# New due times, leads and leanings for a planned order of the same operations: a state-space convolution beside Hedgehog linear attention

## The chip, the cores and the metric

The kernel runs on one core of a Trainium2 chip. The core has four engines that compute, each with its own in-order queue: TensorE (PE, with its weight loads shown apart as PEld), VectorE (DVE), ScalarE (ACT) and GpSimd (POOL). SyncE (SP) issues all of this kernel's transfers, in order. The metric is the device time of one execution in microseconds (us).

## What is computed

Two heads work on inputs of 2048 rows and 576 columns, and their results stand side by side. Head A is an S4D convolution: a filter K for each of 576 channels, made from 128 complex exponentials, convolved over the length with u by a Fourier transform. Head B is Hedgehog linear attention with 32 heads of 18 columns.

```python
# A
dt = jnp.exp(log_dt)
A = -jnp.exp(log_A_real) + 1j * A_imag
C = (C_real + 1j * C_imag) * dt[:, None]
P = jnp.exp((A * dt[:, None])[:, :, None] * pos[None, None, :])
K = 2.0 * jnp.einsum("dn,dnl->dl", C, P).real
y = jnp.fft.irfft(jnp.fft.rfft(u_t, L2) * jnp.fft.rfft(K, L2)[None], L2)[:, :, :L]
a = y.transpose(0, 2, 1) + u * D_skip[None, None, :]
# B
q, k, v = x @ wqkv, split in heads
pq, pk = q and k of each head times w_phi
phi = concatenate([softmax(p), softmax(-p)])          # for pq and pk
kv, z = phi_k^T v, sum over rows of phi_k
o = (phi_q kv) / (phi_q z + 1e-6)
b = o as (rows, 576) @ wo
```

## The kernel before

The work is cut in units, and a planner puts the operations of all units in one order. The units are:

- **fold** 0 and 2: the key's and the query's projection multiplied with w_phi (five blocks, through tiles named e, E and kvb); fold 1 and 3: wv and wo (three parts each; wo's through three tiles e). Each part is loaded, copied to a rounded half wh by ACT (L497, L513) and its rest to wl by DVE or POOL (L498, L514).
- **key** 0 to 15: 128 rows each. The rows are loaded and split (steps without a name, and xd, which stores the split rows for later), multiplied with the folded weights (PE, L431, the helper that records every matmul), passed through the two softmaxes (DVE L568 to L582, POOL L579, ACT L576; step k1, k2) and accumulated into a PSUM tile (k3, k4). **kv** turns the sum into the operand of the queries.
- **query** 0 to 15: the split rows are read back (L536), multiplied, passed through the softmaxes (step q1, q2), transposed (q3), multiplied with kv and divided (q4), transposed again (q5) and multiplied with wo (q6).
- **u** 0 to 15: the first step of the transform of u (u1), kept in DRAM. It takes a tile zi.
- **mags**, **sel**, **par** 0 to 5: the filter's parameters. **group** 0 to 17: two groups of 16 channels each. POOL makes phases (L883 to L888), ACT their sine and cosine (step g1; L898, L903, L904), PE and ACT the magnitudes (g2; L918), DVE multiplies them in (g3; L924 to L929), PE makes the filter (g4) into a tile ks.
- **kfirst** 0 to 3: the first step of the transform of a quarter of the filter, through four tiles zi, stored to DRAM (L950). A quarter needs nine groups.
- **product** 0 to 15: eight for each half of the channels. It loads ff (L988), ub (L995), fk and kb (L1016, L1018), transforms u (p1), multiplies with the filter's transform (p2, p3) and transforms back (p4), storing to DRAM (L1054). The products of a half need all of u and two quarters of the filter.
- **last** 0 to 15: eight for each half. It loads a tile zi (L1064), which needs every product of its half, makes the last step of the transform (l1) and stores the result (L1078).

The planner knows an estimated cost of each operation and walks forward in time. Among the operations that are ready for an engine it takes the one that is due first; the due time of an operation is that of its unit in WANT less the LEAD of its step (the sixth entry of an operation), so a larger LEAD means earlier:

```python
self.ops.append([eng, cost, fn, deps, bufs, self.now - early - LEAD.get(self.part, 0.0), table, ...])
key = (s + late if s + late > at[e] + NEAR else at[e], ops[k][5] + (STAY if e == "pe" and ops[k][10] != mode else 0.0), k)
```

NEAR is the time within which a start counts as at once. STAY is added to the due time of a matmul that needs another tiling of PE than the last one had; TURNOVER to the start of an ACT operation that needs another function table. Some operations may go to either of two engines ("any": ACT or DVE; others DVE or POOL): the engine that ends it first is taken, with LEAN_ACT or LEAN_POOL added to DVE's end.

Tiles come from tags with few buffers. For all but PSUM a tag is strict: its tiles are ranked by the due times of the operations that use them, and a tile may not take a buffer that one of an earlier rank still needs.

```python
for k in sorted(range(n), key=lambda k: ops[k][5]):
    for b in ops[k][4]:
        if id(b) not in place:
            place[id(b)] = seen[b.tag]
...
before = p - low[tag] - more
if before >= self.window[tag]:
    return None
if before and self.strict[tag] and before - sum(v < p for v in ahead[tag]) >= len(fr):
    return None
```

The tags that matter here: zi has 2 buffers (fold 1, u, kfirst, last), e has 3 (the parts of fold, the softmaxes of keys and queries), v1 2 (keys, the parts of sel), x9 3 (the split rows). Where the planner foresees that PE would wait, it puts filler matmuls on a zero tile in front of the next one (L215), so that PE's clock stays up.

Of the kernel before, what the change touches and what calls it, by code (L numbers as in the profile page):

```python
# [158 lines left out]
class Plan:  # L159
# [26 lines left out]
    def op(self, eng, cost, fn, r=(), w=(), with_=(), early=0.0, table=None, busy=1.0, lock=False, mode=(128, 128), add=None):  # L186
# [16 lines left out]
        fill = [add] if add else fill  # L203
        self.ops.append([eng, cost, fn, deps, bufs, self.now - early - LEAD.get(self.part, 0.0), table, busy, lock and eng, (self.unit, early, self.part), mode, fill[0] if fill else None, alt, add])

# [170 lines left out]
def c_dma(nbytes, run=4096):  # L376
# [3 lines left out]


FLEX = "dve", "pool"
STAY, TURNOVER, NEAR, LEAN_POOL, LEAN_ACT = 2.8232, 86.2691, 108.9723, -101.9467, 54.4707
LEAD = dict(g1=890.9031, g2=620.0778, g3=192.8580, g4=207.1228, k1=216.0814, k2=-118.1697, k3=-65.4639, k4=-547.2126, l1=-1073.5691, p1=-946.0003, p2=-42.8734, p3=-112.1202, p4=-277.0577, q1=6.7377, q2=-167.0245, q3=-16.4915, q4=-253.9455, q5=-371.4825, q6=-501.1500, u1=950.3189, xd=-230.4561)
FILL = 114.0


WANT = dict(
    ident=[1001.5195],
    fold=[-6117.3543, -7207.7506, -340.8826, -248],  # L390
    start=[-3485.651],
    key=[-5200.524, -857.2856, -3283.7984, -2041.2554, -2036.0389, -1264.7043, -10155.3465, -4286.2764, -2911.8045,
          -2558.4292, -1360.1364, -2657.9782, -3095.7741, -2082.143, -907.5394, -211.7701],
    kv=[-444.8623],
    query=[1690.5431, 4124.6299, 4143.7194, 1995.4459, 2673.1544, 2389.5478, 1349.1511, 3409.721, 207.6882, 445.7265,
          3385.202, 806.1601, 2667.4484, 3524.0524, 3569.4059, 3651.1724],
    u=[-2745.6629, -420.1168, 204.104, -1422.0066, -3363.2519, 366.0833, -11691.5594, -445.6771, -220.033, -1000.4812,
          -1001.382, -3135.6904, -1460.411, -4014.0618, -2618.6448, 469.9849],
    mags=[-6043.0357],
    sel=[-7319.891, -11916.8894, -3931.5985],  # L400
    dsk=[331.8456],
    par=[-7693.8238, -4634.0292, -1718.349, 81.9699, 1301.2247, 2220.1341],
    group=[-4512.8072, -5429.8639, -4985.5845, -4145.1561, -2678.7949, -1878.2961, -914.9546, -2232.1852, -1467.543,
          -90.2167, -293.4502, -856.2089, 82.9071, 239.3902, 1222.1458, 1540.0762, 1647.3815, 309.0567],
    kfirst=[-2505.5117, -1015.4687, -401.9894, 856.7455],
    product=[1228.5589, 1255.9756, 1206.883, 59.9875, 440.7206, -16.8928, 1079.6264, 659.7095, 1486.7365, 2093.1899,
          2182.0643, 1480.5801, 3075.8325, 2134.1925, 2348.2184, 2387.2577],
    last=[1039.7028, 583.559, 59.784, 2209.6938, 1958.6146, 1737.3942, 2116.436, 1850.9013, 2710.0021, 2371.1266,
          2120.546, 2972.9234, 2398.2107, 3055.0304, 2543.6038, 2544.8052],
)  # L410


# [694 lines left out]
```

## Time and profile before

| | us |
|---|---|
| median of three runs | 597.67 |
| the three runs | 593.55, 597.67, 597.73 |
| the profiled execution | 596.77 |
| its span, first to last instruction | 595.0 |

All rows of the profile are of that one execution. In a row of groups stands the line, engine, operation, tiles (written <- read), shapes and count, then the busy time and mean duration, then the idle time ahead of it and what ended it. In a row of windows stands the window, then busy time (and count) of PE, PEld, DVE, ACT and POOL, the granted share of PE's clock, the DMA engines' busy share and GB/s. In the chain of waits and in a timeline stands the start, the duration and what ran.

### The profile page before, as it was taken

The page shows a single profiled execution, that of the slowest core. Times are in us where ns is not written, and L with a number is a line of the kernel's source. Part 1 is how long each engine was busy: PE and PEld are TensorE (multiplying, and loading weights), DVE is VectorE, ACT ScalarE, POOL GpSimd, SP SyncE. Part 2 cuts the span into 40 slices and gives each one's busy share as a digit, 9 for nine tenths or more (in the row PEclk, how much of TensorE's full clock was granted, in tenths as well). Part 3 has the DMA queues.
Part 4 walks back from the last instruction along what each step waited for, and adds up shares of the span by engine and source line. Part 5 has one row for each costly group of instructions (what it writes and reads, how often), then busy time and mean ns, then how long its engine had stood idle before and what let it go on. Part 6 is the DMA issues. An engine that isn't in the chain of part 4 may idle for free.

```text
span 595.0 us, 19001 instructions
## 1 busy us (share of the span) xinstructions
PE 566.4 (95%) x7794; PEld 468.6 (79%) x7794; DVE 517.7 (87%) x1106; ACT 385.8 (65%) x663; POOL 252.4 (42%) x397
## 2 busy tenths in 40 slices
PE   4999989999999998999999999999999999999996
PEld 3998889999978687898786876766787966777974
DVE  4799899999999996899999999899996789677751
ACT  4479766679596987669668586986965434432332
POOL 0438376685762825943462448545710122011100
PEclk9899999999999999999999999999999999999999
DMA  8979912542048697025666746876529799997687
GB/s 264 280 249 310 332 43 64 191 131 89 9 161 219 196 298 200 1 92 140 190 221 202 254 122 207 239 243 216 156 51 309 188 308 341 308 296 259 198 240 200
DMA packets 91317, 119.26 MB, mean 200 GB/s; under 512 B 9826, under 2 KB 73186, under 8 KB 91230
## 3 DMA queue, kind: packets, MB, share of 16 engines
q1 hardware_dynamic: 91230, 118.04, 63.9%
q8 instruction: 61, 1.00, 0.7%
q14 instruction: 26, 0.21, 0.1%
HBM read 68.76 MB, written 49.26 MB: 198 GB/s over the span
## 4 chain that ended last, share of the span: by engine, by line
PE 63%; DVE 18%; DMA 12%; ACT 3%; issue 2%; SPq 1%; POOL 1%; ACTq 0%; DVEq 0%
PE ps L431 57%; DMA zi<-dram 3%; PE ps L215 3%; DVE ac L450 2%; PE ps L678 2%; DVE cs L924 2%; DMA zo<-in_xT_dram 2%; DVE E L925 2%; DMA e<-in_wo_dram 2%; DMA e<-in_wqT_dram 1%; DMA e<-in_wkT_dram 1%; DVE E L927 1%; DVE E L929 1%; DVE e L446 1%; DMA out_dram<-yo 1%
## 5 line engine op out<-in xcount | busy, mean ns | idle before, releaser
L431 PE MATMUL ps<-wh,x 128*128 128x288 f32 (+2 forms) x1008 | 241.3, 320 | 4.0 <-DMA x<-xd 2.1
L431 PEld LDWEIGHTS ps<-wh,x 128*128 128x128 f32 x1008 | 173.3, 189 | 15.9 <-issue 4.3
L431 PE MATMUL ps<-wl,x 128*128 128x288 f32 (+2 forms) x560 | 175.1, 313 | 0.0
L888 POOL TENSOR_TENSOR cs<-cs,pi 128x128 int32<-128x128 int32 (+4 forms) x180 | 118.5, 661 | 10.1
L431 PEld LDWEIGHTS ps<-wl,x 128*128 128x128 f32 x560 | 105.8, 189 | 0.5
L579 POOL TENSOR_TENSOR o<-e 128x576 f32<-128x576 f32 x32 | 43.1, 1350 | 60.7 <-ACT e L576 54.8
L918 ACT ACTIVATE ps<-ps 128x512 f32<-128x512 f32 x108 | 56.5, 582 | 5.3 <-PE ps L431 5.0
L446 POOL TENSOR_TENSOR ac<-ac 128x288 f32<-128x288 f32 x28 | 22.3, 803 | 75.2 <-DVE ac L450 75.1
L924 DVE TENSOR_TENSOR cs<-ps,cs 128x1024 f32<-128x1024 f32 x36 | 43.7, 1213 | 5.1 <-ACT ps L918 4.8
L215 PE MATMUL ps<-ident,zero 128*32 128x256 bf16 (+6 forms) x330 | 42.9, 281 | 2.7 <-DVE ident L464 1.6
L450 DVE TENSOR_TENSOR ac<-us,ps 128x576 f32<-128x576 f32 x64 | 44.6, 746 | 1.0 <-ACT fT L436 0.5
L431 PEld LDWEIGHTS ps<-kvb,fT 126*128 126x128 f32 (+1 forms) x320 | 38.6, 188 | 6.5 <-issue 2.2
L925 DVE TENSOR_TENSOR E<-ps,cs 128x1024 f32<-128x1024 f32 x36 | 43.5, 1208 | 0.0
L431 PEld LDWEIGHTS ps<-E,cs 128*32 128x32 f32 x2304 | 34.9, 110 | 10.3 <-issue 4.0
L431 PE MATMUL ps<-E,cs 128*32 128x64 f32 x2304 | 41.3, 221 | 1.5 <-DVE E L929 1.0
L431 PE MATMUL ps<-kvb,fT 126*128 126x133 f32 (+1 forms) x320 | 41.5, 279 | 0.7 <-DVE small L571 0.7
L576 ACT ACTIVATE e<-e 128x1152 f32<-128x1152 f32 x32 | 37.1, 1172 | 7.4 <-DVE e L446 6.8
L904 ACT ACTIVATE cs<-cs,hp 128x1040 f32<-128x1040 f32 x36 | 41.4, 1149 | 0.0
L898 ACT ACTIVATE cs<-cs 128x1040 f32<-128x1040 int32 x29 | 31.2, 1074 | 14.9 <-POOL cs L888 14.8
L436 ACT ACTIVATE ot<-ps 128x288 f32<-128x288 f32 x28 | 11.5, 411 | 44.5 <-PE ps L431 44.4
L215 PEld LDWEIGHTS <-zero 128*32 128x32 bf16 (+6 forms) x330 | 32.1, 102 | 10.2 <-issue 4.2
L568 DVE TENSOR_REDUCE small<-ps 128x16 f32<-128x288 f32 (+2 forms) x64 | 28.7, 449 | 12.0 <-PE ps L431 11.2
(140 smaller groups left out, 1077.9 us busy)
## 6 DMA issues: line engine op xcount, KB each, us to landing
xd<-x SPq DMA_DIRECT2D x16, 576.0 KB, 6.0
dram<-zi SPq DMA_DIRECT2D x16, 576.0 KB, 3.8
x<-xd SPq DMA_DIRECT2D x16, 576.0 KB, 4.4
dram<-zi SPq DMA_DIRECT2D x32, 288.0 KB, 3.4
kb<-dram SPq DMA_DIRECT2D x32, 288.0 KB, 4.6
ub<-dram SPq DMA_DIRECT2D x32, 288.0 KB, 3.9
dram<-zo SPq DMA_DIRECT2D x32, 288.0 KB, 4.3
zi<-dram SPq DMA_DIRECT2D x16, 576.0 KB, 5.2
```

What stands on the lines that cost most here:

```text
L215: self.matmul(t[0:cols, 0:n], self.zero.t[0:rows, 0:cols], self.data.t[0:rows].bitcast(BF16)[:, 0:n], start=not o[13], stop=not o[13], ski ...
L431: pe.matmul(o, l, r, start=start, stop=stop, skip_group_check=skip)
L450: op(eng, c_dve(n) if eng == "dve" else c_pool(n), lambda: e.tensor_tensor(dst(), a(), b(), op=alu), r=r, w=w, lock=eng == "pool" or not a ...
L568: op("dve", c_dve(DH * m), lambda: dve.tensor_reduce(ends.t[:, :, 0], v(), axis=AX.X, op=ALU.max, negate=True), r=[p], w=[ends])
L576: op("act", c_act(1152) + 40, lambda: act.activation(e.t, e.t, AF.Exp), r=[e], w=[e], table="exp")
L579: op("pool", c_pool(470), lambda: pool.tensor_tensor(pair.t, e.t[:, :, :, 0:9], e.t[:, :, :, 9:18], op=ALU.add), r=[e], w=[pair], lock=True)
L888: op("pool", c_pool(2 * n * W), lambda n=n, j=j: pool.tensor_tensor(x()[:, :, :, n:2 * n], x()[:, :, :, 0:n], pi.t[:, j:j + 2, gs].bitcast ...
L898: op(("act", "dve"), (c_act(65 * W), c_dve(65 * W)), lambda e, cs=cs, x=x: act.activation(cs.t[:, 0], x(), AF.Abs) if e == "act" else dve. ...
L904: act.activation(cs.t[:, 0], cs.t[:, 0], AF.Sin, scale=-TURN, bias=hp.t)
L918: op("act", c_act(512), lambda: act.activation(ps.t, ps.t, AF.Exp), r=[ps], w=[ps], table="exp")
L924: op("dve", c_dve(64 * W), lambda: dve.tensor_tensor(F(), both(M.t), F(), op=ALU.mult), r=[M, cs], w=[cs])
L925: op("dve", c_dve(64 * W), lambda: dve.tensor_tensor(E.t[:, :, :, 32:64], both(up.t), cs.t[:, :, :, 0:32], op=ALU.mult), r=[up, cs], w=[E])
```

## The change

The program's operations stay the same. Other values are put in for STAY, TURNOVER, NEAR, the two leanings, all LEADs and all due times in WANT.

```diff
--- before.py
+++ after.py
@@ -380,33 +380,33 @@
 
 
 FLEX = "dve", "pool"
-STAY, TURNOVER, NEAR, LEAN_POOL, LEAN_ACT = 2.8232, 86.2691, 108.9723, -101.9467, 54.4707
-LEAD = dict(g1=890.9031, g2=620.0778, g3=192.8580, g4=207.1228, k1=216.0814, k2=-118.1697, k3=-65.4639, k4=-547.2126, l1=-1073.5691, p1=-946.0003, p2=-42.8734, p3=-112.1202, p4=-277.0577, q1=6.7377, q2=-167.0245, q3=-16.4915, q4=-253.9455, q5=-371.4825, q6=-501.1500, u1=950.3189, xd=-230.4561)
+STAY, TURNOVER, NEAR, LEAN_POOL, LEAN_ACT = 37.6104, 135.5510, 109.2559, -92.0902, 57.9818
+LEAD = dict(g1=1412.5796, g2=445.7536, g3=858.8018, g4=859.8314, k1=227.1989, k2=29.9342, k3=83.2118, k4=-331.8215, l1=-1032.4912, p1=-505.0832, p2=172.0822, p3=6.0949, p4=-304.5765, q1=56.1909, q2=-209.9832, q3=-272.1636, q4=-311.2748, q5=-352.9193, q6=-792.7688, u1=840.3076, xd=385.3628)
 FILL = 114.0
 
 
 WANT = dict(
-    ident=[1001.5195],
-    fold=[-6117.3543, -7207.7506, -340.8826, -248],
-    start=[-3485.651],
-    key=[-5200.524, -857.2856, -3283.7984, -2041.2554, -2036.0389, -1264.7043, -10155.3465, -4286.2764, -2911.8045,
-          -2558.4292, -1360.1364, -2657.9782, -3095.7741, -2082.143, -907.5394, -211.7701],
-    kv=[-444.8623],
-    query=[1690.5431, 4124.6299, 4143.7194, 1995.4459, 2673.1544, 2389.5478, 1349.1511, 3409.721, 207.6882, 445.7265,
-          3385.202, 806.1601, 2667.4484, 3524.0524, 3569.4059, 3651.1724],
-    u=[-2745.6629, -420.1168, 204.104, -1422.0066, -3363.2519, 366.0833, -11691.5594, -445.6771, -220.033, -1000.4812,
-          -1001.382, -3135.6904, -1460.411, -4014.0618, -2618.6448, 469.9849],
-    mags=[-6043.0357],
-    sel=[-7319.891, -11916.8894, -3931.5985],
-    dsk=[331.8456],
-    par=[-7693.8238, -4634.0292, -1718.349, 81.9699, 1301.2247, 2220.1341],
-    group=[-4512.8072, -5429.8639, -4985.5845, -4145.1561, -2678.7949, -1878.2961, -914.9546, -2232.1852, -1467.543,
-          -90.2167, -293.4502, -856.2089, 82.9071, 239.3902, 1222.1458, 1540.0762, 1647.3815, 309.0567],
-    kfirst=[-2505.5117, -1015.4687, -401.9894, 856.7455],
-    product=[1228.5589, 1255.9756, 1206.883, 59.9875, 440.7206, -16.8928, 1079.6264, 659.7095, 1486.7365, 2093.1899,
-          2182.0643, 1480.5801, 3075.8325, 2134.1925, 2348.2184, 2387.2577],
-    last=[1039.7028, 583.559, 59.784, 2209.6938, 1958.6146, 1737.3942, 2116.436, 1850.9013, 2710.0021, 2371.1266,
-          2120.546, 2972.9234, 2398.2107, 3055.0304, 2543.6038, 2544.8052],
+    ident=[662.8542],
+    fold=[-7687.5453, -7745.6125, 259.817, 535.0881],
+    start=[-2611.6173],
+    key=[-6803.1211, -230.1406, -1365.6963, -2159.2507, -2013.4955, -1452.8544, -2939.3499, -2827.6947, -5050.6309,
+          -2518.8535, -2118.4827, -2650.666, -9070.313, -995.7874, -2373.4398, -987.9414],
+    kv=[-786.7682],
+    query=[3770.3533, 3016.2205, 509.4875, 2846.8004, 1491.4103, 3693.7243, 3988.4128, 4713.0274, 1842.5362,
+          2601.4694, 2059.0315, 4163.9131, 979.8723, 550.1266, 4637.1683, 3978.4516],
+    u=[-2652.5344, -1884.6824, -2759.9008, -2536.1968, -519.4906, -1715.5344, 61.2931, -1133.0048, -3905.8435,
+          -3179.3226, -79.6233, -3423.2365, -3284.4628, -4491.6778, -2694.6224, -12210.2772],
+    mags=[-6932.6723],
+    sel=[-4531.7687, -13025.2225, -9048.6714],
+    dsk=[-1454.0969],
+    par=[-8082.5413, -6080.3201, -1900.8545, 318.5964, 1347.4086, 2335.0621],
+    group=[-5429.9062, -5502.1674, -5990.1496, -4902.2989, -4185.1114, -2837.5423, -3314.4141, -2894.5059, -2718.3579,
+          -1748.4322, -1071.7324, -831.957, -412.4379, 1066.8302, 1224.9381, 1181.0338, 1103.1102, 2326.0027],
+    kfirst=[-3805.4915, -1483.2884, -573.9485, 1243.6831],
+    product=[1234.4685, -154.0236, 1747.233, 70.1659, 1226.8661, 949.6933, 49.7659, 1059.5957, 2418.1186, 3443.8845,
+          3102.0019, 2360.5039, 2005.2384, 3993.9616, 1947.1217, 2343.6319],
+    last=[873.1326, -129.3535, 2214.046, 737.0179, 504.8954, 188.1562, 1822.1782, 642.4446, 4235.0692, 3659.2532,
+          3501.5163, 3991.4065, 3676.1068, 2821.8987, 3937.8348, 3122.3667],
 )
 
 
```

## The prediction

> **What bounds the kernel now.** I read the page first (busy shares, slices, chain), then busy time by windows cut where the slices change, then the fillers, the chain of waits in order of time, and last the timelines of SP, PE and DVE at the places where the chain leaves PE and DVE.
>
> ```profile
> span 595.0 us, 19001 instructions
> PE 566.4 (95%) x7794; PEld 468.6 (79%) x7794; DVE 517.7 (87%) x1106; ACT 385.8 (65%) x663; POOL 252.4 (42%) x397
> DVE  4799899999999996899999999899996789677751
> DMA  8979912542048697025666746876529799997687
> PE 63%; DVE 18%; DMA 12%; ACT 3%; issue 2%; SPq 1%; POOL 1%; ACTq 0%; DVEq 0%
> ```
>
> The sum below is made against this execution: 596.77 us with a span of 595.0, 0.9 below the median of 597.67 us. PE looks full everywhere, but part of that is filler. The next answer gives the busy time of the filler matmuls alone (PE, PEld, DVE, granted clock, DMA share, GB/s), the one after it that of all work:
>
> ```profile
> 0.00:75.00 75.00, 11.63 (x79) 8.70 (x79) 0.11 (x1) 0.95 0.90 288
> 75.00:450.00 375.00, 29.97 (x242) 22.60 (x242) 0.00 (x0) 1.00 0.52 158
> 450.00:595.00 145.00, 1.33 (x9) 0.84 (x9) 0.00 (x0) 0.99 0.84 265
> ```
> ```profile
> 0.00:14.20 14.20, 6.66 (x42) 5.01 (x42) 6.44 (x18) 7.18 (x11) 0.79 (x10) 0.94 0.85 259
> 14.20:75.00 60.80, 60.73 (x486) 55.60 (x487) 52.67 (x132) 44.74 (x74) 29.50 (x45) 0.96 0.91 295
> 75.00:225.00 150.00, 144.81 (x2553) 128.77 (x2552) 145.89 (x287) 111.88 (x181) 91.92 (x146) 1.00 0.46 140
> 225.00:250.00 25.00, 22.30 (x247) 20.23 (x250) 19.13 (x39) 17.66 (x27) 17.53 (x20) 1.00 0.36 101
> 250.00:456.00 206.00, 200.00 (x3041) 158.89 (x3031) 199.89 (x416) 156.15 (x260) 97.74 (x164) 1.00 0.60 185
> 456.00:557.00 101.00, 99.78 (x1201) 73.69 (x1202) 77.34 (x180) 36.07 (x88) 12.29 (x12) 1.00 0.87 277
> 557.00:595.00 38.00, 32.08 (x247) 26.42 (x245) 16.36 (x41) 12.15 (x25) 2.62 (x2) 0.97 0.72 212
> ```
>
> So there are three regimes. Up to 75 us transfers feed a full PE. From 75 to 456 us DVE is the limit: it idles 4.1 us in 75 to 225 (150 - 145.89), 5.9 us in 225 to 250 and 6.1 us in 250 to 456, while PE runs 30 us of filler. From 456 us on (the last group of the filter is done there) PE is the limit, with hardly any filler, and DVE idles 23.7 us, then 21.6 us. An order of the same operations cannot shorten the work; it can only take idle time from DVE before 456 us, or move PE work from after 456 us into the time that filler takes now.
>
> **What the new numbers change.** I sorted the due times of both versions by hand (WANT less the LEAD of the part) and looked at what buffers with a strict order (zi 2, e 3, v1 2, x9 3) make of them, since a tile there may not be taken ahead of one that is due earlier.
>
> *The start.* Before: sel 1, u 6, key 6, par 0, sel 0, fold 1, fold 0, mags, group 1, key 0. After: sel 1, u 15, key 12, sel 2, par 0, fold 1, fold 0, mags, key 0. Units of one kind are alike, so this is one order under other names. In zi, six u units stand ahead of kfirst 0, seven more ahead of kfirst 1 and three ahead of kfirst 2, in both versions. The third part of sel is fifth in v1 in both. PE's long wait stays as it is:
>
> ```profile
> PE ps L431 <- DMA e<-in_wkT_dram: 6.0, 1, 6.0
> ```
>
> Cost 0, between -1 and +1.
>
> *The fold of wo.* Before, fold 3 (-248) takes its three e tiles ahead of every query, the first of which is due at 201 (208 - 6.7). After, query 2 (509 - 56 = 453) and query 13 (494) come ahead of fold 3 (535). The hole at 225 to 250 us is made of this:
>
> ```profile
> 220.73 10.62 DMA e<-in_wo_dram
> POOL wl L514 <- ACT wh L513: 6.8, 2, 4.4
> 224.50 0.46 DVE L568 TENSOR_REDUCE small<-ps 128x16 f32<-128x288 f32 x1 [0.17 <-PE ps L431]
> 232.87 0.46 DVE L450 TENSOR_TENSOR e<-ps,small 128x288 f32<-128x288 f32 x1 [2.94 <-POOL wl L514]
> 239.40 1.22 DVE L924 TENSOR_TENSOR cs<-ps,cs 128x1024 f32<-128x1024 f32 x1 [2.40 <-ACT ps L918]
> ```
>
> DVE takes the first query's maxima at 224.50, yet it writes its e only at 232.87, since all three e tiles hold parts of wo that wait for a transfer, then ACT, then POOL. ACT, in order, stands behind the same transfer, and the exponentials that the group's multiplication at 239.40 wants come late. The two DVE waits are 5.3 us of the window's 5.9. With two queries ahead, both have their cover; wo itself comes later, so that the first output products wait, but PE has filler to give there. I take -4 us: most of the 5.3, with something left for ACT still meeting a late transfer. Bounds 0 (the hole moves behind query 13) and -5.9.
>
> *The last step of half 0 and kfirst 3.* In zi the order was last 2 (60), last 1 (584), the four tiles of kfirst 3 (857), then six more lasts. Now it is last 1, 5, 4, 7, 3, 0 (-129 to 873), then kfirst 3 (1244), then two. All lasts of half 0 need every store of the products of half 0. Before, this ended so:
>
> ```profile
> 444.37 5.70 DMA dram<-zo
> 450.14 5.66 DMA zi<-dram
> 455.93 1.19 PE ps L431 x8
> 459.54 1.36 PE L431 MATMUL ps<-ks,w 32*64 32x288 f32 x32
> 461.84 10.66 SPq L950 DMA_DIRECT2D dram<-zi  x8
> ```
>
> The products' store landed at 450.1, two zi tiles were filled, PE read them at 455.9, and kfirst 3 began at 459.5. After, four more lasts are meant to lie in the DVE-bound time. One takes PE 1.19 us, so PE after 456 us has 4 x 1.19 = 4.8 us less to do, in place of filler. Their copies go to ACT as easily as to DVE. For this the products must finish earlier, and their due times say so: the second step of p1 goes from 929 to 2202 (median 1816) to 351 to 2252 (median 1510), while the queries' q1 moves about 100 later. I take -4.8 us; the bounds are +13 (rival below) and -4.8.
>
> *Leads of the groups* (g1 +522, g2 -174, g3 +666, g4 +653): DVE takes a group's multiplications ahead of more key and query work, and groups 13 to 16 move from between 46 and 1454 to between 208 and 366 in that step; group 17 goes the other way, from 116 to 1467. As DVE is full there, this orders its work and does not remove any. The keys' later steps (k2 to k4, 148 to 216 earlier) and l1 and u1 (41 earlier, 110 later) are of the same kind. I take 0, for the 4.1 + 6.1 us of idle time in 75 to 225 and 250 to 456 are short waits behind ACT and PE that a new order makes anew. Bounds: -10.2 if none came back, +4 if as much again came.
>
> *Late queries* (q3 to q6 later), *xd* (616 earlier), *dsk* and *ident*: the queries still end beside the lasts, two of them due after the last product's p1 (4022 before, 4499 now), as before. Cost 0; if that cover went, the tail's transfers (5.98 and 6.54 us below) would stand bare.
>
> *STAY, TURNOVER, NEAR, LEAN.* STAY (2.8 to 37.6) decides only between units due within 38 of each other; its price is part of PEld's wait for issue below, taken as 0. TURNOVER (86 to 136) spaces table loads on ACT, which idles 49.9 of 206 us in 250 to 456: 0 while ACT has that room, 1.28 us each without it. The leans move 10 and 3.5 ns against differences of hundreds: a wide multiplication that changes sides takes 1158 ns off DVE and puts 1528 on POOL. One or two may move, -1 to +1, taken as 0.
>
> ```profile
> PEld ps L431 <- issue: 28.6, 75, 6.3
> L903 ACT ACT_TABLE_LOAD x14 | 18.0, 1283 | 0.2
> L446 DVE TENSOR_TENSOR e<-e,small 128x1152 f32<-128x1152 f32 (+1 forms) x28 | 32.4, 1158 | 0.2
> L446 POOL TENSOR_TENSOR e<-e,small 128x576 f32<-128x576 f32 (+1 forms) x4 | 6.1, 1528 | 23.4 <-DVE small L450 23.3
> SPq L988 <- PE ps L431: 37.7, 12, 15.9
> ```
>
> The last row is SP's own queue: a product's ff load waits at its head, up to 15.9 us, and the transfers due after it wait too. The order of all issues changes with the due times, so such a wait may land on a load that PE wants; that is in the +4 above.
>
> **The sum:** 596.8 - 4 - 4.8 = 588.0 us.
>
> **Rivals.**
>
> *Given back.* DVE's waits come back elsewhere, and kfirst 3 waits just long enough to eat what the lasts gave. For it: 12% of the chain is transfers, whose real times no order of due times knows. Against it: both places are named and single. 596 us.
>
> *Slower: kfirst 3 stuck behind six lasts.* The tail shows how fast lasts go through two zi tiles:
>
> ```profile
> 557.72 2.22 SPq L1064 DMA_DIRECT2D zi<-dram  x2
> 580.27 0.33 SPq L1064 DMA_DIRECT2D zi<-dram  x1
> 574.55 5.98 DMA out_dram<-yo
> 581.86 6.54 DMA zi<-dram
> ```
>
> Two tiles in (580.27 - 557.72) / 3 = 7.5 us. If the products' last store still lands at 450.1, kfirst 3 starts at 450.1 + 3 x 7.5 = 472.6 and not at 459.5: 13 us later, and with it products and lasts of half 1. Queries fill PE meanwhile, but then they are missing in the tail. It decides when the store lands less than 22.5 us ahead of the last group's matmuls. For it: by DVE's own due times the last product (product 2, p2 at 1575) now comes after four queries, where it came after three (1299). 596.8 - 4 + 13 = 606 us.
>
> *Much faster.* Every wait of DVE between 75 and 456 us goes (16.1 us) and the lasts give their 4.8: 576 us. For it, the fillers show room; against it, those waits are many and short.
>
> *A cold PE.* Row: the granted clock is 0.94 and 0.96 up to 75 us, where PE waited once for 6.0 us, and 1.00 in the next four windows, where no wait of that length stands. A wait like it in mid-kernel, not foreseen and so without filler, would cost at least some slow matmuls: 0.06 x 14.2 + 0.04 x 60.8 = 3.3 us by the two early windows, 588 + 3.3 = 591.3 us. The Trainium skill (TensorE: Matmul & The Clock Gate, What's actually happening) has the clock halved after an idle window of some 3.4 us; by that rule a changed order that bares one long wait would pay about 1.7 us beside it, an estimate from that page (3.4 us at half speed), and come to 589.7. The trace agrees as far as it goes: no window of mid-kernel has such a wait, and none is below 1.00.
>
> **How the numbers follow.** A measurement of this kernel tells about 1% from no change. Forecast 588: 0.42 (of it 0.34 below 591.7, 0.08 within 1%), its own range 582 to 595. Given back: 0.26 (0.03, 0.20, and 0.03 slower). Slower: 0.13 (0.02 within, 0.11 over 603.6). Much faster: 0.14. Cold PE: 0.05 (0.02, 0.03). Faster 0.34 + 0.03 + 0.14 + 0.02 = 0.53, same 0.33, slower 0.14. The range goes from 576 to 603: it leaves out 0.11 above (the slower rival) and, as 576 is the middle of the much faster one, 0.07 below.
>
> **What would show it.** In the changed kernel's windows, DVE idles under 2 us where the queries begin, and the first e of a query comes before POOL's L514. In SP's timeline four or more zi loads of the lasts stand ahead of the stores of kfirst 3. Filler in mid-kernel falls below 30 us by about 5, and the stretch from the last group to the end (139 us) shortens by about 5. Wrong would be: a wait of kfirst 3's copies or stores for zi, DVE's busy share before the last group unchanged at 97%, or a tail in which lasts run without a query beside them.

## The result, and the profile after

| | before | after |
|---|---|---|
| median of four runs of each on one chip, us | 597.70 | 587.49 |
| the runs lie between, us | 593.55 and 598.11 | 587.25 and 588.19 |
| the profiled execution / its span, us | 596.77 / 595.0 | 587.27 / 585.5 |
| last group's multiplication (L924), us | 452.5 | 450.3 |
| last store of the products of half 0 (L1054) issued, us | 444.4 | 426.7 |
| stores of kfirst 3 (L950), first and last, us | 461.8, 471.8 | 458.9, 470.5 |
| last store of the products of half 1, us | 555.1 | 545.7 |
| from there to the end, us | 39.9 | 39.8 |

The ratio is 0.985, with a 95% interval of 0.980 to 0.989. The change is faster, by 10.2 us in the medians (597.70 - 587.49) and by 9.5 us in the span of the profiled executions (595.0 - 585.5).

The page of the changed kernel:

```profile
span 585.5 us, 18811 instructions
PE 558.6 (95%) x7694; PEld 461.4 (79%) x7694; DVE 516.7 (88%) x1110; ACT 392.5 (67%) x672; POOL 239.3 (41%) x385
...
DVE  4799999999999899999899999999978788787751
PE 59%; DVE 19%; DMA 9%; ACT 8%; issue 2%; POOL 1%; SPq 1%; ACTq 0%; DVEq 0%
```

PE is as full as before (95%) with 7.8 us less to do (566.4 to 558.6). POOL lost 12 instructions and 13.1 us, DVE gained 4 and ACT 9. Transfers have 9% of the chain, where they had 12%. Busy time by the same windows (PE, PEld, DVE, ACT, POOL, clock, DMA share, GB/s):

```profile
75.00:225.00 150.00, 147.02 (x2548) 129.45 (x2548) 145.56 (x293) 118.90 (x190) 85.23 (x142) 1.00 0.45 140
225.00:250.00 25.00, 21.80 (x267) 20.20 (x266) 23.01 (x47) 16.80 (x25) 16.35 (x24) 0.93 0.34 114
250.00:456.00 206.00, 197.58 (x3018) 154.51 (x3018) 195.19 (x406) 158.83 (x269) 91.72 (x152) 1.00 0.67 203
456.00:557.00 101.00, 100.84 (x1164) 76.89 (x1160) 82.67 (x194) 37.52 (x88) 13.54 (x13) 1.00 0.83 251
557.00:585.50 28.50, 23.04 (x180) 19.14 (x178) 9.78 (x23) 8.21 (x20) 1.31 (x1) 0.96 0.78 239
```

DVE's idle time in 225 to 250 fell from 5.9 to 2.0 us. After 456 us PE idles 0.2 us until 557, and 0.5 us in all until 580; then only the last copies and stores are left. So the end is set by how much PE work is left at 456 us. The next four answers split that: first PE's busy time after 456 us of all work, then that of the matmuls of the lasts alone (they read a tile zi), before and then after. The columns are PE, clock, DMA share and GB/s.

```profile
456.00:595.00 139.00, 131.87 (x1446) 0.99 0.83 259
...
456.00:595.00 139.00, 18.95 (x128) 0.99 0.83 259
```
```profile
456.00:585.50 129.50, 123.88 (x1341) 0.99 0.82 248
...
456.00:585.50 129.50, 11.91 (x88) 0.99 0.82 248
```

PE's work after 456 us shrank by 8.0 us (131.87 - 123.88), its idle time by 1.5 us (7.1 to 5.6); together that is the 9.5 us. Of the 8.0, the lasts are 7.0 (18.95 - 11.91) and filler is the 1.3 us that stood there; the other work is 0.4 us more. Before, PE ran the 128 matmuls of the 16 lasts after 456 us (two of them start just ahead of it); now 40 of them, five lasts, lie earlier. At 1.19 us each these five are 6.0 of the 7.0 us; the 11 lasts that stayed take 1.1 us less (several run in pairs, 16 matmuls in 2.16 us, where two single lasts take 2 x 1.19). What they replaced is filler, here PE's L215 in 75 to 225, 225 to 250 and 250 to 456, before and after:

```profile
75.00:225.00 150.00, 10.07 (x83) 1.00 0.46 140
225.00:250.00 25.00, 6.85 (x55) 1.00 0.36 101
250.00:456.00 206.00, 13.05 (x104) 1.00 0.60 185
```
```profile
75.00:225.00 150.00, 7.97 (x59) 1.00 0.45 140
225.00:250.00 25.00, 3.51 (x25) 0.93 0.34 114
250.00:456.00 206.00, 9.01 (x67) 1.00 0.67 203
```

Filler before 456 us fell by 2.1 + 3.3 + 4.0 = 9.4 us. The lasts did not take the filler's own place: in 430 to 456, where they run, there were 0.5 us of it before. The rest of the filler went earlier, where products and steps of queries moved up; up to 456 us PE runs as many matmuls of every other kind as before, but for 64 more of the last group (0.5 us) and 8 transposes fewer (1.1 us). The lasts then took the time that this work had left. SP's own timeline of the changed kernel shows the new order:

```profile
425.48 1.59 SPq L1054 DMA_DIRECT2D dram<-zo  x2
431.26 0.81 SPq L1064 DMA_DIRECT2D zi<-dram  x2
437.26 0.32 SPq L1064 DMA_DIRECT2D zi<-dram  x1
...
449.07 0.33 SPq L1064 DMA_DIRECT2D zi<-dram  x1
458.87 3.71 SPq L950 DMA_DIRECT2D dram<-zi  x4
```

Six loads of lasts stand ahead of kfirst 3: two from 431.26 on and one each at 437.26, 439.34, 446.92 and 449.07. They have 28 us for it (431.26 to 458.87), since the products of half 0 were stored 17.7 us earlier (444.4 to 426.7), and kfirst 3 is still 3 us earlier than before.

The place where the queries begin shows what the filled hole cost in its turn. The timelines of DVE, POOL and PE in the changed kernel:

```profile
224.99 0.45 DVE L450 TENSOR_TENSOR e<-ps,small 128x288 f32<-128x288 f32 x1
...
236.84 0.17 DVE L450 TENSOR_TENSOR small<-small 128x32 f32<-128x32 f32 x1
237.89 2.20 DVE L450 TENSOR_TENSOR small<-small 128x32 f32<-128x32 f32 x1
```
```profile
229.40 2.26 POOL L514 TENSOR_TENSOR wl<-e,wh 128x960 fp32r<-128x960 f32 x1 [2.01 <-ACT wh L513]
237.57 2.48 POOL L514 TENSOR_TENSOR wl<-e,wh 128x960 fp32r<-128x960 f32 x1 [0.21 <-ACT wh L513]
```
```profile
241.65 0.50 PE L215 MATMUL ps<-ident,zero 128*128 128x256 bf16 x2 [2.42 <-DVE cs L924]
```

The first query's e now comes at 224.99, before any L514 of POOL. But a DVE multiplication that took 0.17 us at 236.84 took 2.20 us at 237.89, and ended (240.09) when POOL's difference of wo did (237.57 + 2.48 = 240.05). So 2.0 us of the "busy" DVE in this window is standing still. The Trainium skill (SBUF — State Buffer, SBUF: two separate sides) says that a DVE operation with two SBUF inputs and a GpSimd operation that reads SBUF take turns on one pair of ports, each locked for its whole instruction; the trace agrees. The same operation takes 2.20 and 2.21 us in runs 5 and 8 below, which keep this order. PE, held by the multiplication behind it, idled 2.42 us, even its filler.

### The profile page after: what moved, and what is told of

The parts are those of the page before. It is cut to its first block, busy times and chain, and to the rows that moved or that the text cites. A ratio compares the mean times of both kernels' runs of the same rounds, so it can differ in the third digit from the quotient of the medians.

```text
span 585.5 us, 18811 instructions
## 1 busy us (share of the span) xinstructions
PE 558.6 (95%) x7694; PEld 461.4 (79%) x7694; DVE 516.7 (88%) x1110; ACT 392.5 (67%) x672; POOL 239.3 (41%) x385
## 4 chain that ended last, share of the span: by engine, by line
PE 59%; DVE 19%; DMA 9%; ACT 8%; issue 2%; POOL 1%; SPq 1%; ACTq 0%; DVEq 0%
PE ps L431 55%; DVE cs L924 2%; DVE E L925 2%; DMA zi<-dram 2%; PE ps L215 2%; PE ps L678 2%; DVE e L446 1%; DVE ac L450 1%; ACT cs L904 1%; DMA kb<-dram 1%; DMA e<-in_wkT_dram 1%; DVE E L927 1%; ACT cs L903 1%; DVE E L929 1%; DMA dt<-in_ldt_dram 1%
## 5 line engine op out<-in xcount | busy, mean ns | idle before, releaser
L924 DVE TENSOR_TENSOR cs<-ps,cs 128x1024 f32<-128x1024 f32 x36 | 43.6, 1212 | 5.5 <-ACT ps L918 5.4
L431 PEld LDWEIGHTS ps<-kvb,fT 126*128 126x128 f32 (+1 forms) x320 | 40.2, 196 | 7.2 <-PE ps L431 1.7
L898 ACT ACTIVATE cs<-cs 128x1040 f32<-128x1040 int32 x35 | 37.6, 1073 | 10.7 <-POOL cs L888 10.5
L431 PE MATMUL ps<-kvb,fT 126*128 126x133 f32 (+1 forms) x320 | 42.8, 285 | 0.9 <-DVE small L571 0.6
L446 POOL TENSOR_TENSOR ac<-ac 128x288 f32<-128x288 f32 x21 | 17.2, 826 | 63.8 <-DVE ac L450 63.8
L215 PE MATMUL ps<-ident,zero 128*128 128x256 bf16 (+6 forms) x230 | 33.1, 292 | 6.5 <-DVE cs L924 4.3
L903 ACT ACTIVATE cs<-cs 128x1040 f32<-128x1040 int32 x36 | 38.3, 1064 | 0.2
L436 ACT ACTIVATE zi<-ps 128x288 f32<-128x288 f32 x73 | 25.1, 417 | 16.1 <-PE ps L431 15.6
```

The lines of the kernel that those rows point to most:

```text
L215: self.matmul(t[0:cols, 0:n], self.zero.t[0:rows, 0:cols], self.data.t[0:rows].bitcast(BF16)[:, 0:n], start=not o[13], stop=not o[13], ski ...
L431: pe.matmul(o, l, r, start=start, stop=stop, skip_group_check=skip)
L898: op(("act", "dve"), (c_act(65 * W), c_dve(65 * W)), lambda e, cs=cs, x=x: act.activation(cs.t[:, 0], x(), AF.Abs) if e == "act" else dve. ...
L903: act.activation(cs.t[:, 1], cs.t[:, 1].bitcast(I32), AF.Sin, scale=TURN)
L924: op("dve", c_dve(64 * W), lambda: dve.tensor_tensor(F(), both(M.t), F(), op=ALU.mult), r=[M, cs], w=[cs])
```

## The experiments

Each time is a median on one chip beside the kernel before, which came to 597 to 598 us each time; a ratio is to that. Runs 1 to 4, 5 to 8 and 9 to 12 ran on three chips, and the changed kernel was not run again beside them; run 8, which keeps its order up to some 545 us, came to 587.4 us. The table has where each run's stages fell, from one profiled execution each (us; label shortened to its number). Stages of one order differ between executions: the changed kernel and runs 5, 8 and 9 have the same order up to some 430 us, and their last group comes at 450.3, 450.5, 449.3 and 454.9 us. So a difference of 2 us in this table is not clear of that.

| | last group L924 | kfirst 3's first store | products end | span | products' end to the end |
|---|---|---|---|---|---|
| before | 452.5 | 461.8 | 555.1 | 595.0 | 39.9 |
| after | 450.3 | 458.9 | 545.7 | 585.5 | 39.8 |
| 1 | 454.9 | 464.0 | 565.5 | 606.6 | 41.1 |
| 2 | 479.3 | 487.9 | 582.1 | 620.5 | 38.4 |
| 3 | 475.4 | 483.9 | 589.8 | 628.5 | 38.7 |
| 4 | 451.9 | 472.1 | 571.8 | 611.6 | 39.8 |
| 5 | 450.5 | 459.3 | 554.3 | 594.8 | 40.5 |
| 6 | 453.3 | 462.5 | 551.5 | 591.3 | 39.9 |
| 7 | 456.4 | 465.4 | 558.3 | 599.2 | 40.8 |
| 8 | 449.3 | 457.9 | 545.7 | 584.8 | 39.0 |
| 9 | 454.9 | 463.2 | 557.4 | 597.3 | 39.9 |
| 10 | 457.3 | 467.1 | 559.0 | 598.8 | 39.7 |
| 11 | 486.9 | 495.7 | 591.5 | 629.8 | 38.3 |
| 12 | 455.4 | 463.8 | 558.2 | 604.8 | 46.7 |

### Due times changed, and the order planned anew

Run 1 takes the changed kernel and gives four lasts due times behind kfirst 3:

```diff
+ WANT["last"][4] = 1260.0; WANT["last"][7] = 1300.0; WANT["last"][3] = 1340.0; WANT["last"][0] = 1380.0
```

> The changed kernel with the due times of lasts 4, 7, 3 and 0 set behind kfirst 3 (1260 to 1380, kfirst 3 at 1244), so that two lasts of half 0 stand ahead of it, as before the change. The order is the same up to some 430 us. Two places (my theory): the four lasts return to the part that PE bounds, 4 x 1.19 = 4.8 us: 587.5 + 4.8 = 592.3, 591 to 594, the stretch from the last group to the end 5 us longer. Small drift (rival: the gain is a sum of many small differences, and neither place has a price of its own): 587.5, within 1.5.

605.1 us (599.4 to 609.8), ratio 1.011 (1.007 to 1.016), 17.6 above the changed kernel. The four lasts stand behind kfirst 3 again, but the planner, walking on from there, also spread the queries anew, and after 557 us PE has 14.2 us of filler, where the changed kernel has none. The run mixes the two.

Runs 2 and 3 move wo: ahead of queries 2 and 13 in the changed kernel, and behind the first queries in the kernel before.

```diff
+ WANT["fold"][3] = 300.0    # 2, in the changed kernel
+ WANT["fold"][3] = 460.0    # 3, in the kernel before
```

> The changed kernel with fold 3 due at 300 and not 535, ahead of the first two queries, as before the change; all that comes after some 205 us is ordered anew. Two places: the hole where the queries begin comes back, DVE idles 4 us more between 215 and 250 us, and the time is 587.5 + 4 = 591.5 (589.5 to 593.5). Small drift: 587.5, within 3, whatever the hole does.

> The kernel before with fold 3 due at 460 and not -248, behind the first two queries, and nothing else. Two places: DVE idles 4 us less where the queries begin, and the time is 597.7 - 4 = 593.7 (591.5 to 595.5). Small drift: 597.7, within 3.

Run 2: 621.2 us, ratio 1.039 (1.035 to 1.042). Run 3: 629.6 us, 1.053 (1.050 to 1.056). The window 225 to 250 in runs 2 and 3 (all engines):

```profile
225.00:250.00 25.00, 23.60 (x292) 21.55 (x290) 23.66 (x47) 17.05 (x25) 17.09 (x22) 1.00 0.32 110
```
```profile
225.00:250.00 25.00, 20.04 (x200) 18.07 (x200) 20.40 (x40) 18.14 (x27) 15.91 (x19) 0.96 0.36 101
```

In run 2 DVE idles only 1.3 us there (25 - 23.66), less than in the changed kernel, and yet the last group comes 29 us later. In run 3 it idles 4.6 us (25 - 20.40), 1.3 less than before, and the time is 32.5 us longer (629.57 - 597.07). In neither does the state of the hole go with the time. One due time can change every choice behind it, and what that costs hides what the run was meant to show.

Run 4 gives the kernel before only the changed kernel's due times of products and lasts and the leads of p1 to p4 and l1.

> The kernel before with the due times of products and lasts and the leads p1 to p4 and l1 of the changed kernel, and nothing else; five lasts of half 0 stand ahead of kfirst 3. The order is the same up to some 300 us. Two places: 597.7 - 4.8 = 592.9 (591 to 595). Small drift: 597.7, within 3. Slower rival of the prediction (kfirst 3 stuck behind the lasts): 600 or more, with kfirst 3's first matmul after 465 us.

615.9 us, ratio 1.031 (1.028 to 1.035). SP's timeline in run 4:

```profile
443.35 1.52 SPq L1054 DMA_DIRECT2D dram<-zo  x2
446.99 0.86 SPq L1064 DMA_DIRECT2D zi<-dram  x2
454.77 0.32 SPq L1064 DMA_DIRECT2D zi<-dram  x1
...
467.82 0.33 SPq L1064 DMA_DIRECT2D zi<-dram  x1
472.09 1.26 SPq L950 DMA_DIRECT2D dram<-zi  x2
```

This is the slower rival: the products are stored when they were before (443.8 us after 444.4), the lasts take the two zi tiles, and kfirst 3's first matmul runs at 470.3, its first store at 472.1; the rival had worked out 472.6 for its start. So these due times alone do not bring the products forward; with the other due times as they were they block.

Runs 11 and 12 are the control: the changed kernel and the one before, every due time in WANT shifted at random by up to 20 either way, where the values span some 15000.

> The changed kernel with every due time of its units shifted at random by up to 20 up or down (their range is some 15000), so that the planner orders anew. Theory A: the order is a fine balance that the values hold and that no single rule gives; any small shift that changes early decisions costs 15 to 35 us, as the three runs with one or two due times changed (605, 616, 630): 603 to 623 us. Theory B: those runs were slow for what was moved, and a random shift of this size stays within 4 us of 587.5.

> The kernel before with the same kind of random shift of up to 20; its order is the same until about 300 us. Theory A (fine balance): 608 to 630 us, and the last group comes later than 458 us. Theory B (a shift of this size does nothing by itself): 594 to 602 us.

Run 11: 632.7 us, ratio 1.059 (1.056 to 1.062). Run 12: 602.8 us, 1.010 (1.006 to 1.013). In run 11 DVE idles 12.6 us in 75 to 225 (150 - 137.41), where it idled 4.4 in the changed kernel, and 13.4 in 250 to 456 (206 - 192.59).

Run 11 is slower by 45 us (632.7 - 587.5): the direction is theory A's, the size is beyond its range. Run 12 is slower by 5.9 us (602.84 - 596.98), closer to B's 602 than to A's 608, and its last group (455.4) comes ahead of A's 458. In the changed kernel a shift without any meaning thus costs more than the meant ones, so runs 1 and 2 say nothing of what they moved. In the kernel before the one shift tried costs less than runs 3 and 4 (32.5 and 18.9 us); a single shift can't tell whether those losses are due to what was moved. Run 4 is read by its timeline, not by its time.

### The order kept, and single operations moved

From here on, but for run 8, the planner's sequence is written down, with its fillers, and only the named operations are moved in it, left out or given other tiles. Three dots in the code stand for lines not shown. Run 5 takes the changed kernel and puts the lasts 4, 7, 3 and 0 behind kfirst 3, each by 40.5 to 43 us of the plan's time (the numbers are ns):

```diff
+    units = {('last', 4): 43000.0, ('last', 7): 42500.0, ('last', 3): 41000.0, ('last', 0): 40500.0}
...
```

> The changed kernel's program order, held fast, in which only the operations of lasts 4, 7, 3 and 0 are moved: from ahead of kfirst 3 to behind it, among the first products of half 1. Nothing else is ordered anew (in e1 the planner ordered all that follows anew). PE work (my theory): 4 x 1.19 us return to the stretch that PE bounds: 587.5 + 4.8 = 592.3 (591 to 594). Chain of the filter head (rival that the first runs suggest: the time is the last store of the products of half 1 plus 39 us, and what stands between kfirst 3 and the products delays them by its place in SP's queue and its transfers, 0.86 MB each at some 300 GB/s): 587.5 + 4 x 2.9 = 599. Small drift: 587.5 within 1.5.

596.9 us (590.8 to 599.4), ratio 0.998 (0.995 to 1.001): nearly the whole gain is gone. The windows of run 5 (all engines):

```profile
440.00:456.00 16.00, 13.66 (x203) 12.78 (x204) 13.66 (x26) 7.65 (x13) 3.74 (x3) 0.97 0.47 135
456.00:470.00 14.00, 13.29 (x153) 10.94 (x146) 9.64 (x27) 5.39 (x14) 2.89 (x2) 0.91 0.56 144
...
485.00:530.00 45.00, 42.04 (x524) 27.73 (x524) 32.08 (x73) 17.31 (x43) 4.86 (x5) 1.00 0.98 322
```

And PE alone after 456 us, all of its work and the lasts':

```profile
456.00:594.80 138.80, 129.22 (x1380) 0.98 0.80 253
...
456.00:594.80 138.80, 16.18 (x112) 0.98 0.80 253
```

Against the changed kernel, PE has 5.3 us more to do after 456 us (129.22 against 123.88, of it 4.3 the lasts, 24 matmuls or three lasts more; the sixth had been read after 455.7 us already) and idles 4.0 us more (138.8 - 129.22 = 9.6 against 5.6): 9.3 us, the whole difference of the spans. Of the idle time, 3.0 us are in 485 to 530, where the DMA engines are at 0.98, and 0.7 in 456 to 470. Ahead of 456 us, at 452, no last covers PE any more: it idles 2.0 us and the clock then falls. The sequence holds no filler for that place (it has 9.3 us of filler in 250 to 456, as the changed kernel's 9.0), so a planner might have lost less.

Run 6 takes the kernel before and leaves the lasts 3, 4, 6 and 7 out.

```diff
+    left_out = [("last", n) for n in (3, 4, 6, 7)]
+    seq = [x for x in seq if self.ops[x[0]][9][0] not in left_out]
```

> The kernel before with its program order held fast and lasts 3, 4, 6 and 7 of half 0 left out (their rows of the result are not written). PE work: 597.7 - 4.8 = 592.9 (591 to 594). Chain: the products of half 1 end 9 us earlier, as they do in the changed kernel, 588. Small drift: 597.7 within 1.5.

592.0 us, ratio 0.991 (0.988 to 0.994): 5.9 us for four lasts (597.85 - 591.99), against 4.8 for their matmuls. In its profiled execution PE's work after 456 us is 4.7 us less than before (131.87 - 127.16), which is the price of those matmuls.

Run 9 is run 5 with the result tiles yo of the lasts of half 0 in other buffers:

```diff
+            if o[9][0] in [("last", n) for n in range(8)] and b.tag == "yo":
+                b.tag = "cs"
```

> The order of the changed kernel is kept operation by operation, lasts 4, 7, 3 and 0 stand behind kfirst 3 as in the run where they were moved back (596.86 us), and the result tiles yo of the lasts of half 0 are taken from the tag cs (4 buffers, free by then) instead of yo. That run was 9.4 us above the changed kernel (596.86 - 587.49), of which the four lasts' own PE work is 4.8 us by the prediction's row and 5.7 us by the run that left four of them out. Theory A: the rest, 3.7 to 4.6 us, is the wait of their copies for the yo tiles to be stored (the rows of a wait for out_dram<-yo, 6.2 and 3.5 us). Then it comes to 587.5 + 4.8 to 5.7 = 592.3 to 593.2 us, and those rows are gone. Theory B: the rest is the transfers themselves, which share 485 to 530 us with the products' loads at a DMA share of 0.95 and more; then it stays at 595 to 598 us, and PE still idles about 3 us there.

596.3 us, ratio 0.998 (0.995 to 1.002). The copies' waits for stored yo tiles are gone, and the median stays: the time is theory B's. The executions lie between 591.3 and 599.9, though, four of them at 591.3 to 592.6, and the profiled one is among the slow ones (599.12). In it PE idles 1.7 us in 485 to 530, in place of 3.0, at the same DMA share of 0.98, and not B's 3; another 3.1 us lie in 456 to 470. So the waits for yo are not worth the 3.7 to 4.6 us that theory A gave them; that the transfers are the cause isn't shown.

Run 8 gives the lasts of half 1 four zi buffers (tag cs) in the changed kernel, to see if the tiles set the 39 us of the tail.

```diff
- yo, zi = B("yo", [128, 2, HD]), B("zi", [128, 4, HD])
+ yo, zi = B("yo", [128, 2, HD]), B("cs" if half else "zi", [128, 4, HD])
```

> The changed kernel with the tiles of the lasts of half 1 taken from the tag cs (four buffers, free by then) in place of zi (two); the order is the same up to some 545 us. Chain: the 39 us from the last product's store to the end are four pairs of transfers at 7.5 us through two tiles; with four tiles they shorten, down to what PE has to do there (23 of 28.5 us busy): 587.5 - 4 = 583.5 (582 to 585.5). PE work alone: 587.5, as PE has its queries there anyway.

587.4 us, ratio 0.984 (0.980 to 0.988), as the changed kernel. The tail does not hang on the tiles: PE is what fills it, in the changed kernel too, where it is busy 22.7 of the 23 us from 557 to 580.

Runs 7 and 10 try to fill the hole in the kernel before. Run 7 puts the three parts of wo in tiles of the tag ac. Run 10 puts two of them there and moves ACT's three copies and POOL's three differences behind the first two queries' exponentials.

```diff
# run 7
+            if o[9][0] == ("fold", 3) and b.tag == "e":
+                b.tag = "ac"
# run 10
+    place = dict(act=[233000, 233000, 233000], pool=[235500, 239500, 244400])
...
+    e[1].tag = e[2].tag = "ac"
```

> The kernel before with its program order held fast; only the three parts of wo are loaded into tiles named ac, which are free then, so that the first query's softmax needn't wait for an e. Hole theory: the wait of 2.9 us of DVE at 230 us goes, groups and all that follows come 3 us earlier: 594.7 (593.5 to 596). Rival: the next wait (the exponentials behind ACT) takes it up again, 597.7 within 1.5.

> The order of the kernel before is kept operation by operation, except that the second and third part of wo go to tiles of the tag ac (free by then) and that ACT's three copies of wo and POOL's three differences stand behind the first two queries' exponentials. So the queries' e waits for no part of wo, ACT stands at no transfer of wo ahead of the group's exponentials, and no load is held on SP. Theory A (the prediction's step: the hole at 225 to 250 us is worth most of 5.3 us): DVE idles under 3 us in 225 to 250, the last group comes 3 to 5 us earlier (448 to 450 us instead of 453), and the time is 593 to 595 us. Theory B (the 5 us come back on DVE or at kfirst 3, whose zi tiles wait for the products' stores anyway): the hole closes but the last group or kfirst 3 is less than 1.5 us earlier, and the time is 596 to 599 us.

Run 7: 600.7 us, ratio 1.004 (1.001 to 1.006). The query's e no longer waits, but the third load of wo waits for a buffer of ac and holds the next query's rows behind it on SP:

```profile
PE ps L431 <- DMA x<-xd: 5.5, 1, 5.5
```

Run 10: 599.9 us, ratio 1.004 (1.002 to 1.007). No wait for wo is left, and the group's multiplication of 239.40 comes at 236.43. But then the waits of ACT and of DVE in that place are for others:

```profile
ACT ay L827 <- DMA cim<-in_cim_dram: 2.7, 1, 2.7
```
```profile
DVE small L568 <- PE ps L431: 3.2, 4, 1.3
DVE cs L924 <- ACT ps L918: 3.0, 1, 3.0
```

DVE is busy 17.30 us in 225 to 250, less than the 19.13 before. The last group is 4.8 us later, not earlier. Theory A's sign, DVE idle under 3 us, isn't met, and B's premise, a closed hole, isn't either. What a closed hole is worth by itself remains open.

## Why the prediction was right, and where its steps were not

The total came as forecast: 588.0 against 587.5 us, a sum of -8.8 against -9.5 in the span. Its parts did not come as they were sized, and that their errors nearly cancel is luck: one term was too small, and the other can't be found in the time that it was to save.

*The last step of half 0 and kfirst 3, -4.8.* The mechanism is right and shown: six loads of lasts ahead of kfirst 3, filler replaced, PE work after 456 us less (123.9 us in place of 131.9, and 124.4 in run 8, which keeps the order). The term was too small. It counted four lasts of 1.19 us by the order in zi. The two that stood ahead of kfirst 3 before were read by PE only from 455.9 us on, so they too lay in the PE-bound stretch, and five lasts moved out of it: 6.0 us by their matmuls, 7.0 with the shorter time of those that stayed. From the last group's multiplication to the end it is now 135.2 us, after 142.5. Putting four of them back cost 9.4 us (run 5), leaving four out of the old order gave 5.9 (run 6); these are two estimates of what the placement is worth. Above the matmuls, run 5 shows PE bare at 452 us with a slow clock behind it, and idle at a DMA share of 0.98. The waits for yo don't explain it (run 9); the other causes weren't taken apart.

*The fold of wo, -4.* The hole closed as described: DVE idles 1.99 us, and the first e comes before POOL's L514. The step that failed is the one from there to the time. Of the 3.9 us that the idle time lost, 2.0 are a DVE operation that stands behind POOL's moved difference of wo, and PE's 2.42 us wait there was followed by a slow clock in this execution. The groups, 3.5 us ahead of the hole (214.28 against 217.81), were 8.2 ahead in it (231.25 against 239.40) and 4.8 at the next group (240.39 against 245.16). The last group came only 2.2 us earlier. DVE's busy time (third column) from 75 us to the last group, before and after:

```profile
75.00:453.00 378.00, 365.04 (x5807) 306.03 (x5806) 361.92 (x737) 283.70 (x464) 207.19 (x329) 1.00 0.53 160
75.00:450.00 375.00, 360.40 (x5729) 299.15 (x5729) 358.10 (x734) 290.90 (x475) 190.04 (x314) 1.00 0.56 170
```

Its share is unchanged, 95.7% before (361.92 of 378) and 95.5% after (358.10 of 375). The prediction named that as a sign that it was wrong, and for this step it is (its 97% is the share of the two long windows alone). In all DVE idles 16.1 us before and 16.9 after: the 3.9 us that the hole lost came back behind it, where DVE idles 10.5 us from 250 us to the last group (16.9 - 4.4 - 2.0), after 6.1. The rival that has the waits given back was right about this step. The last group is earlier because DVE has 3.8 us less to do ahead of it (361.92 - 358.10), while ACT has 7.2 more. All of the change but the place of the four lasts, this term included, comes to 1.0 us by run 5 (597.85 - 596.86) and to 4.5 us by run 6 (591.99 - 587.49), each with an interval of 2 to 3 us either way. How much of it is the hole isn't shown.

*Leads of the groups, 0.* DVE idles 4.4 us in 75 to 225, as before (4.1), so the leads removed no work. But PE's filler there fell by 2.1 us, and the groups were 3.5 us ahead before the hole, in this execution. What that is worth isn't shown; it is part of the 1.0 to 4.5.

*The start, late queries, STAY and the rest, 0.* PE's long wait at the start is 5.1 us after 6.0. The products' end and the end are 39.8 us apart, after 39.9. Nothing here speaks against zero.

*The slower rival* was a real mechanism, and its condition fits the runs: the products' last store had to land 22.5 us ahead of kfirst 3. In the changed kernel's chain it lands at 431.2, and PE's timeline begins kfirst 3 at 456.83, 25.6 us later:

```profile
426.69 4.51 DMA dram<-zo
```
```profile
455.71 1.19 PE L431 MATMUL ps<-zi,w 128*64 128x288 f32 x8
456.83 1.36 PE L431 MATMUL ps<-ks,w 32*64 32x288 f32 x32
```

Run 4 has the store issued at 443.8 and landed at 446.9, kfirst 3's first matmul at 470.3, and 615.9 us: a loss of 19, where the rival had 13 (and 606 us, with the -4 in it). What brought the store forward by 17.7 us in the changed kernel is the one thing that the sum needed and that no run isolated: the due times of products and lasts alone don't do it.

*A cold PE.* It came in part: one fall to half clock in mid-kernel, at 241.9 us. The order alone doesn't make it: runs 5 and 8 have the same wait of 2.42 us in the same place and no fall (last section).

## What to carry to other kernels

Find the moment from which one engine is full until the end, and count that engine's work on either side of it by busy time, not by the order in a queue: what leaves the far side is the gain, and what takes its place on the near side must have been filler or idle. Before work is pulled ahead of a shared buffer, look at when its own input lands, since the same reordering with a late input costs more than it could give. To test one step of a searched order, keep the sequence and move single operations; a planner run again with a random nudge of its inputs moved these kernels by 6 and by 45 us. And look for time that a new wait took back: DVE's hole closed here, and its idle time as a whole stayed.

## What the runs showed of the hardware

*PE's clock fell after a shorter wait than expected.* The prediction had only a wait of 6.0 us to go by. In the changed kernel, after the wait of 2.42 us that ended at 241.65 (PE alone: busy time, clock, DMA share, GB/s):

```profile
241.00:242.00 1.00, 0.35 (x3) 0.89 0.50 74
242.00:243.00 1.00, 1.00 (x6) 0.50 1.04 353
```

Run 8 has the same operations there, and the same wait of PE, which ended at 243.96; the clock stays up:

```profile
243.96 0.38 PE L215 MATMUL ps<-ident,zero 128*128 128x256 bf16 x2 [2.42 <-DVE cs L924]
```
```profile
243.00:244.00 1.00, 0.04 (x1) 1.00 0.36 38
244.00:245.00 1.00, 1.00 (x10) 1.00 0.86 280
```

In run 5 it stays up too, behind the same 2.42 us. Run 10, after a wait of only 1.40 us from 223.0 to 224.4:

```profile
224.00:225.00 1.00, 0.58 (x5) 1.00 1.05 218
...
226.00:227.00 1.00, 1.00 (x6) 0.50 0.99 262
```

The kernel before has a wait of 1.91 us, and the clock stays up behind it:

```profile
234.00:235.00 1.00, 0.15 (x1) 1.00 0.02 9
235.00:236.00 1.00, 1.00 (x8) 1.00 0.06 16
```

Run 6 keeps that order, has 1.97 us in the same place, and 0.50 behind it.

In the falls of the changed kernel and of run 10 the half clock lasts some 3.4 us (three whole rows at 0.50 and parts of the two beside them, 0.89 and 0.90 in the one, 0.96 and 0.83 in the other), a loss of about 1.7 us. The Trainium skill (TensorE: Matmul & The Clock Gate, What's actually happening) has the clock at half after an idle window of some 3.4 us that runs freely; the length of the slow stretch and the prediction's 1.7 us agree, but the waits ahead of these falls (1.40 and 2.42 us) were shorter than such a window. Waits of 2.42 us and of some 1.9 us were each followed by a fall in one execution and by none in another with the same operations there. So one profile's fall doesn't tell one order from another, and the length of the wait alone doesn't decide it; what does isn't shown.

*The tail is nearly constant.* From the products' last store to the end 13 of the 14 kernels take 38.3 to 41.1 us, in whatever order the rest is; run 12, with 46.7, has 8.1 us of filler after 456 us where the kernel before has 1.3.
